# Three k decays moved to VectorE, and a new schedule of turns and loads, in a chunked linear-attention kernel with an MLP behind it

## The chip, the core and the metric

The kernel runs on one core of a Trainium2 chip. The core has TensorE (PE, matrix products into PSUM), VectorE (DVE), ScalarE (ACT), GpSimd (POOL) and SyncE (SP, here only a queue for DMAs). Each engine works through its own queue in order and waits on semaphores for the others. DMAs are asked for from SP's, ScalarE's and GpSimd's queues. The metric is the device time of one execution, in microseconds (us); lower is better.

## The reference

Four sequences of 768 tokens, 8 heads of 64. Each head has a decay `lam`; within a block of 64 tokens the scores are masked and decayed, and a state of 64 x 64 is carried from block to block. The result, 3072 tokens by 512, goes through an MLP with the activation h * tanh(softplus(h)).

```python
def _attn_ref(q, k, v, lam):
    ...
    for b in range(nb):
        sl = slice(b * block, (b + 1) * block)
        qb, kb, vb = (q[:, :, sl].copy(), k[:, :, sl].copy(), v[:, :, sl].copy())
        intra = np.einsum('bhic,bhjc->bhij', qb, kb) * Dmask[None]
        intra = np.einsum('bhij,bhjd->bhid', intra, vb)
        inter = np.einsum('bhid,bhde->bhie', qb * lam_pow[None], kv_state)
        out[:, :, sl] = intra + inter
        kb_dec = kb * rev_pow[None]
        kv_state = lam_block[None, :, None, None] * kv_state + np.einsum('bhsd,bhse->bhde', kb_dec, vb)
    return out.astype(np.float32)

def _moe_ref(x, w_in, w_out):
    h = x @ w_in
    sp = np.where(h > 20.0, h, np.log1p(np.exp(np.minimum(h, 20.0))))
    g = h * np.tanh(sp)
    return (g @ w_out).astype(np.float32)
```

`w_in` is 512 x 2048, `w_out` 2048 x 512. All inputs and the output are float32 in memory.

## The kernel before

The kernel works with blocks of C = 128 tokens. The state at a block's start carries everything before it, so the block size can be chosen freely. A **chunk** is one block of one of the four sequences, with all 8 heads; chunk i = 4n + b is block n of sequence b. The four chunks of a block make a **group** of 512 tokens; there are NG = 6 groups, n = 0 to 5.

**Stages.** The last loop of the kernel runs over n. Stage n does the MLP products of group n in **units**, and beside them the attention of group n + 1 in **pieces**, which are strewn among the units so that TensorE always has work. A stage from n = 1 on has 30 units: 16 (u = 0 to 15) for the first product with its activation (`mm1_unit`, tile `hsg`), and 14 (u = 16 to 29) for the second product (`fast_unit`: seven half-sized products in two halves each, in place of eight, with sums of tokens, `token_sum` into `gsum`, and of weights, `weight_sum` into `tsum`, made by VectorE). The first unit of stage n + 1 reads all of `xt[n + 1]`, the attention's output of the whole group.

**Pieces.** For groups from n = 2 on, a chunk has three pieces:
- `chunk_a`: TensorE makes k-transposed times v (`pv`), VectorE adds the old state (`raw`), GpSimd multiplies by the block's decay (`w`, the new state); then `turn(i + 2)` where that chunk is of the same group.
- `chunk_s`: TensorE makes the scores from `kraw` and `qraw` into two PSUM banks (tags pS and pk, one buffer each), VectorE masks them into `sb`.
- `chunk_o`: TensorE makes the output from `qraw` and the state, and from `sb` and v; VectorE scales it to `xtok`, and a DMA transpose asked for by SP turns it into `xt`.

Their order is a0 s0 a1 s1 o0 a2 s2 o1 a3 s3 o2 o3. The table `room` says how many pieces follow each unit. In stage 1 they stand at units 9 to 14 and 16 to 21, in later stages at units 4 to 19.

**Turns.** `turn(i)` has k multiplied by its decay (`scale_k`, tile `ktil`; by GpSimd for most chunks), and asks SP for two DMA transposes: q into `qraw`, then the decayed k into `kraw` (four buffers each). SP's queue holds these, the transposes of `xtok` and most output stores, in program order.

**Loads.** `load_k`, `load_q` and `load_v` are DMAs from float32 to float16 asked for by GpSimd, 128 KB each. Those of group 2 are asked for late in stage 0 and at its end. Stages 1 to 3 each ask for the twelve loads of the group two ahead, one at every second unit from u = 1 to 23. They stand in GpSimd's queue in one order with its decays and state updates; `kn`, `qn` and `vz` have eight buffers each.

**Order.** The schedule is written out by hand: each engine's instructions come in the order of the program. At a unit that order is: the unit's own instructions, a load from `later`, weight sums, token sums, a `turn` where one is due, then the pieces.

Lines that matter here: 261 (`scale_k`), 268 (`turn`), 377 (`chunk_a`, its `turn` at the end), 723 (`room`), 739 (`later`), 775 (the `turn` at unit 0 of stage 1). In the profile L264 is the decay, L273 the two turns of q and k, L384/L392/L394 are `pv`, `raw` and `w`, L406/L411 the scores and `sb`, L421/L425/L428/L429 the output, `xtok` and its turn, L482 the first MLP product, L541 `tsum`, L560 `gsum`, L587 the second product, and L69/L77/L80 the loads of k, q and v.

Of the kernel before, what the change touches and what calls it, by code (L numbers as in the profile page):

```python
# [13 lines left out]
def bc(ap, axis, n):  # L14
    shape = list(ap.shape)
    shape.insert(axis, n)
    return ap.unsqueeze(axis).broadcast_to(shape)
# [3 lines left out]
def kernel(  # L21
# [10 lines left out]
    nc = tc.nc  # L32
    B, H, S, D = q.shape
    C = 128
    NG = S // C
# [225 lines left out]
    def scale_k(i):  # L261

        t = work.tile([128, H, D], F16, name="ktil", tag="ktil", bufs=6)
        (nc.vector if i <= B or i >= (NG - 1) * B else nc.gpsimd).tensor_tensor(  # L264
            out=t, in0=kn[i], in1=bc(lk, 2, D), op=ALU.mult)
        ktil[i] = t

    def turn(i):

        scale_k(i)  # L270
        for src, name, to in ((qn, "qraw", qraw), (ktil, "kraw", kraw)):
            to[i] = work.tile([128, JP, C], F16, name=name, tag=name, bufs=4)
            nc.sync.dma_start_transpose(out=to[i], in_=src[i].rearrange("p h c -> p (h c)"))  # L273
# [103 lines left out]
    def chunk_a(s):  # L377

        n, b = s.n, s.b
        i = n * B + b  # L380
        if n < NG - 1:
            pv = ps.tile([128, JP, 128], F32, name="pv", tag=s.spare, bufs=2)
            for j in range(JP):
                nc.tensor.matmul(  # L384
                    pv[:, j, :].rearrange("p (a e) -> p a e", a=2),
                    ktil[i][:, 2 * j : 2 * j + 2, :].rearrange("p h c -> p (h c)"),
                    vz[i % NVB][:, 2 * j : 2 * j + 2, 0:D], start=True, stop=True,
                )
            for hf in range(2):
                raw = work.tile([128, 2, 128], F32, name="raw", tag="raw", bufs=3)  # L390
                hs = slice(2 * hf, 2 * hf + 2)
                nc.vector.tensor_tensor(  # L392
                    out=raw, in0=pv[:, hs, :], in1=wst[b][hf][n % 2], op=ALU.add)
                nc.gpsimd.tensor_tensor(  # L394
                    out=wst[b][hf][(n + 1) % 2], in0=raw, in1=lbm[:, hs, :], op=ALU.mult)
        if i + 2 < (n + 1) * B:
            turn(i + 2)

    def chunk_s(s):
# [32 lines left out]
    def chunk_pieces(n):  # L432
        chunks = []
        for b in range(B):
            s = Chunk()
            s.n, s.b = n, b
            chunks.append(s)
        out_ = []
        for t in range(B + 1):
            if t < B:  # L440
                out_ += [(chunk_a, chunks[t]), (chunk_s, chunks[t])]
            if t >= 1:
                out_.append((chunk_o, chunks[t - 1]))
        return out_
# [14 lines left out]
    def att_pieces(n):  # L459
        halves = att_halves(n)  # L460
        out_ = []
        for t in range(len(halves) + 2):
            if t < len(halves):
                out_.append((att_a, halves[t]))
            if 0 <= t - 1 < len(halves):
                out_.append((att_s, halves[t - 1]))
            if 0 <= t - 2 < len(halves):
                out_.append((att_o, halves[t - 2]))
        return out_
# [6 lines left out]
    def mm1_part(n, ni, lo, hi):  # L476

        if lo == 0:
            ph_t[ni] = ps.tile([128, GT], F32, name="ph", tag="po" if ni == 2 else "ph", bufs=2)
        w = DF // WS // 128  # L480
        for kc in range(NKC):
            nc.tensor.matmul(  # L482
                ph_t[ni][:, lo:hi],
                win0[min(ni, 2)][:, kc, max(ni - 2, 0) * 128 : max(ni - 2, 0) * 128 + 128] if ni < w
                else win[ni // w][:, kc, (ni % w) * 128 : (ni % w) * 128 + 128],
                xt[n][:, kc, lo:hi], start=(kc == 0), stop=(kc == NKC - 1),
            )
# [44 lines left out]
    def weight_sum(i, s):  # L532

        ks = slice(s * NKI // WS, (s + 1) * NKI // WS)
        a, b, op = (
            (w_quarter(0, 1, s), w_quarter(0, 0, s), ALU.subtract),
            (w_quarter(1, 1, s), tsum[0][:, ks, :], ALU.subtract),
            (w_quarter(1, 1, s), w_quarter(0, 1, s), ALU.subtract),
            (w_quarter(1, 0, s), tsum[1][:, ks, :], ALU.subtract),
        )[i]  # L540
        nc.vector.tensor_tensor(out=tsum[i][:, ks, :], in0=a, in1=b, op=op)  # L541
# [165 lines left out]
    for n in range(NG):  # L707
        units = [(mm1_unit, (n, ni)) for ni in range(NKI)]

        if n == 0:  # L710
            units += [(mm2_unit, (n, b2 + b, part)) for b2 in range(0, B, 2) for part in range(WS)
                      for b in range(2)]
        else:
            units += [(fast_unit, (n, step, blk)) for step in range(7) for blk in range(2)]
        pieces = []
        if n + 1 < NG:
            pieces = att_pieces(n + 1) if n + 1 < NT else chunk_pieces(n + 1)
        if n == 0:

            i = max(i for i, (f2, _) in enumerate(pieces) if f2 is att_a)  # L720
            pieces[i : i + 3] = pieces[i + 1 : i + 3] + pieces[i : i + 1]

        if n == 0:
            room = dict(zip(range(24, 32), (1, 2, 3, 3, 3, 3, 3, 3)))
        else:
            first = 8 if n == 1 else 3
            span = (22 if n == 1 else 20) - first
            room = {first + u: (u + 1) * len(pieces) // span - u * len(pieces) // span
                    for u in range(span)}
        if n == 1:  # L730

            for ni in range(3):
                mm1_part(n, ni, 0, GT - C)
                while late and ni < 2:
                    f2, s = late.pop(0)
                    f2(s)
                    if f2 is att_o:
                        break
        later = []
        if 1 <= n < NG - 2:  # L740
            later = [(lambda f=f, i=i: f(i)) for i in range((n + 2) * B, (n + 3) * B)
                     for f in (load_k, load_q, load_v)]
        nl = len(later)
        for u, (fn, args) in enumerate(units):
            rest = fn(*args)
            while later and u >= 1 and (nl - len(later)) * 24 <= (u - 1) * nl:
                later.pop(0)()
            if n == 0 and 19 <= u < 23:
                weight_sum(0 if u < 21 else 2, u % 2)
            if n == 1 and 4 <= u < 8:  # L750
                weight_sum(1 if u < 6 else 3, u % 2)
            if n > 0 and u in (9, 10):
                token_sum(n, 2, u - 9)
            if n > 0 and u == NKI - 3:
                token_sum(n, 0, 0)
            if n > 0 and u == NKI - 2:
                token_sum(n, 1, 0)
            if n > 0 and u == NKI - 1:
                token_sum(n, 0, 1)
                token_sum(n, 1, 1)  # L760
            if n > 0 and u in (NKI + 2, NKI + 3):
                token_sum(n, 3, u - NKI - 2)
            if n == 0 and 2 <= u < 2 + nh:
                att_kv(first_halves[u - 2], "po")
                att_w(first_halves[u - 2])
            if n == 0 and u % 2 == 1 and 0 < (u + 1) // 2 < B:
                scale_k((u + 1) // 2)
            if n == 0 and nh + 2 <= u < nh + 2 + NVB - B:
                nc.vector.memset(vz[u - nh - 2 + B][:, :, D : 2 * D], 0.0)
            if n == 0 and nh + 2 <= u < nh + 2 + NKB:  # L770
                nc.vector.memset(kz[u - nh - 2], 0.0)
            if n == 0 and u == 17:
                q_decays()
            if n == 0 and u == 16:
                nc.vector.tensor_scalar(out=maskT, in0=rel, scalar1=0.0, scalar2=None, op0=ALU.is_ge)
            if n == 0 and u == 18:
                scale_k(B)
            if n == 1 and u == 0:
                turn((n + 1) * B + 1)
            if n > 0 and n + 2 < NG and u in (23, 25):  # L780
                turn((n + 2) * B + (u - 23) // 2)
            for _ in range(room.get(u, 0)):
                f2, s = pieces.pop(0)
                s.spare = "po" if u < NKI - 1 else "ph"
                f2(s)
            if n == 0 and rest:
                rest()
        if n == 0:
            late = pieces
            while ahead:  # L790
                ahead.pop(0)()
# [30 lines left out]
```

## Time and profile before

| | us |
|---|---|
| three runs, median | 215.28 |
| the three runs | 217.44, 214.69, 215.28 |
| the profiled execution, time | 213.99 |
| the profiled execution, span | 211.8 |
| ScalarE busy in the span | 90.2 |

A page line such as `L394 POOL TENSOR_TENSOR w<-raw,lbm ... x24 | 18.6, 798 | ...` gives the line, the engine, the operation, the tile written and the tiles read, the count, the busy time in us, the mean in ns of one, and behind the second bar the engine's idle time ahead of these instructions and what ended it. In the timeline a line begins with the start (us from the span's beginning) and the duration; neighbours of one kind are merged, with their count at the end, and square brackets hold the idle time ahead and its releaser. Matmuls are pipelined, so of several merged ones the time to the next start is the better measure. In the view by window each engine's busy time in a stretch is followed by its count of instructions; the last three numbers are the granted TensorE clock, the share of the DMA engines and GB/s. "Issue" as a releaser means that the profile shows nothing that the engine waited for.

### The profile page before, as it was taken

Reading aid. Unit: us, or ns where it says so; the run is one execution under the profiler, and the core shown is the slowest. Engines: PE = TensorE matmul, PEld = TensorE weight load, DVE = VectorE, ACT = ScalarE, POOL = GpSimd, SP = SyncE. Lnnn points to the kernel's source line nnn. Section 1 sums busy time; section 2 is a strip of 40 time slices with the busy share of each in tenths; the row PEclk is TensorE's granted clock in tenths of the full one; section 3 lists DMA queues with packets and bytes.
Section 4 is the critical chain, followed back from the end, with each engine's and each line's share of the span. In section 5 each row is a group of like instructions: output and inputs, shape, how many; then the busy total and the mean of one; then the engine's idle time right before and its main releaser. Section 6 shows DMA issues by size and latency. Waiting matters only on the chain.

```text
span 211.8 us, 4225 instructions
## 1 busy us (share of the span) xinstructions
PE 198.4 (94%) x1672; PEld 127.8 (60%) x1672; DVE 127.9 (60%) x234; ACT 90.2 (43%) x159; POOL 110.6 (52%) x135
## 2 busy tenths in 40 slices
PE   7798999999997888989999999999999999999993
PEld 2465444577543477834579844579844588644893
DVE  6667560787715978616996517995727675222533
ACT  5474568466664321045532054532065521266310
POOL 7996333999899989608969409966000000000000
PEclk9999999999999999999999999999999999999998
DMA  9999999999999999994999994999963124400014
GB/s 133 141 158 178 206 207 185 155 198 73 179 144 163 134 101 125 138 242 78 118 136 66 163 264 69 112 129 82 234 160 74 25 28 99 152 0 0 2 56 145
DMA packets 112469, 26.75 MB, mean 126 GB/s; under 512 B 102594, under 2 KB 111938, under 8 KB 112450
## 3 DMA queue, kind: packets, MB, share of 16 engines
q0 software_dynamic: 78080, 13.37, 87.5%
q1 hardware_dynamic: 31392, 10.49, 25.7%
q10 hardware_dynamic: 2978, 2.62, 4.1%
q8 instruction: 13, 0.21, 0.4%
q14 instruction: 6, 0.05, 0.1%
HBM read 27.26 MB, written 6.29 MB: 158 GB/s over the span
## 4 chain that ended last, share of the span: by engine, by line
PE 75%; POOL 13%; DMA 6%; DVE 2%; issue 2%; POOLq 0%; DVEq 0%
PE ph L482 32%; PE z L587 13%; PE x L587 7%; PE y L587 7%; PE po L504 7%; DMA win<-in_moe_w_in_dram 4%; POOL kn L69 3%; POOL vz L80 3%; POOL qn L77 3%; DMA kraw<-ktil 2%; PE pS L406 2%; PE fin L587 2%; PE pO L425 2%; PE pO L421 1%; POOL ktil L264 1%
## 5 line engine op out<-in xcount | busy, mean ns | idle before, releaser
L482 PE MATMUL ph<-xt,win 128*128 128x512 f16 (+2 forms) x404 | 90.2, 369 | 2.4 <-issue 1.5
L496 ACT ACTIVATE hsg<-ph 128x512 f16<-128x512 f32 x96 | 57.0, 597 | 69.4 <-PE ph L482 69.3
L482 PEld LDWEIGHTS <-win 128*128 128x128 f16 x404 | 36.3, 98 | 38.9 <-issue 2.7
L587 PEld LDWEIGHTS <-gsum 128*128 128x128 f16 x336 | 31.1, 98 | 3.6
L394 POOL TENSOR_TENSOR w<-raw,lbm 128x256 f16<-128x256 f32 x24 | 18.6, 798 | 21.7 <-DVE raw L392 21.6
L560 DVE TENSOR_TENSOR gsum<-hsg 128x1024 f16<-128x1024 f16 x20 | 18.0, 913 | 13.2 <-ACT hsg L496 13.2
L411 DVE TENSOR_TENSOR sb<-pS,maskT 128x512 f16<-128x512 f32 x32 | 20.5, 683 | 8.1 <-PE pS L406 8.1
L587 PEld LDWEIGHTS <-hsg 128*128 128x128 f16 x240 | 22.9, 98 | 3.4
L77 POOL DMA_DIRECT2D qn<-in_q_dram x23 | 20.8, 904 | 5.5 <-DMA wout<-in_moe_w_out_dram 3.3
L80 POOL DMA_DIRECT2D vz<-in_v_dram x24 | 21.8, 910 | 3.4 <-DMA win<-in_moe_w_in_dram 1.7
L69 POOL DMA_DIRECT2D kn<-in_k_dram x23 | 21.2, 920 | 4.1 <-DMA wout<-in_moe_w_out_dram 1.7
L587 PE MATMUL z<-tsum,gsum 128*128 128x256 f16 x160 | 19.8, 273 | 0.0
L392 DVE TENSOR_TENSOR raw<-pv,w 128x256 f32<-128x256 f32 x24 | 9.1, 416 | 17.4 <-PE pv L384 15.5
L587 PE MATMUL x<-wout,hsg 128*128 128x256 f16 x160 | 19.4, 273 | 0.0
L264 POOL TENSOR_TENSOR ktil<-kn,lk 128x512 f16<-128x512 f16 x15 | 16.8, 1129 | 0.1
L504 PE MATMUL po<-wout,hsg 128*128 128x512 f16 x64 | 15.1, 379 | 0.0
L428 DVE TENSOR_TENSOR xtok<-pO,lqt 128x512 f16<-128x512 f32 x16 | 10.9, 683 | 0.0
L560 DVE TENSOR_TENSOR gsum<-hsg,gsum 128x1024 f16<-128x1024 f16 x10 | 7.6, 764 | 5.2 <-PE z L587 5.2
L264 DVE TENSOR_TENSOR ktil<-kn,lk 128x512 f16<-128x512 f16 (+1 forms) x9 | 6.2, 684 | 6.8 <-DMA kn<-in_k_dram 6.7
L425 PE MATMUL pO<-vz,sb 128*128 128x64 f16 x128 | 9.2, 193 | 0.8 <-DVE sb L411 0.8
L587 PE MATMUL z<-tsum,hsg 128*128 128x256 f16 x80 | 9.5, 272 | 0.0
L504 PEld LDWEIGHTS <-hsg 128*128 128x128 f16 x64 | 5.9, 97 | 5.9
(101 smaller groups left out, 226.5 us busy)
## 6 DMA issues: line engine op xcount, KB each, us to landing
out_dram<-osum SPq DMA_DIRECT2D x14, 256.0 KB, 3.1
vz<-in_v_dram POOLq DMA_DIRECT2D x24, 128.0 KB, 4.8
kn<-in_k_dram POOLq DMA_DIRECT2D x23, 128.0 KB, 5.1
qn<-in_q_dram POOLq DMA_DIRECT2D x23, 128.0 KB, 5.4
wout<-in_moe_w_out_dram POOLq DMA_DIRECT2D x4, 512.0 KB, 16.7
win<-in_moe_w_in_dram POOLq DMA_DIRECT2D x3, 512.0 KB, 10.4
out_dram<-osum ACTq DMA_DIRECT2D x5, 256.0 KB, 3.5
out_dram<-osb ACTq DMA_DIRECT2D x4, 256.0 KB, 5.5
```

What stands on the lines that cost most here:

```text
L69: nc.gpsimd.dma_start(out=kn[i], in_=chunk_rows(k, i))
L77: nc.gpsimd.dma_start(out=qn[i], in_=chunk_rows(q, i))
L80: nc.gpsimd.dma_start(out=vz[i % NVB][:, :, 0:D], in_=chunk_rows(v, i))
L264: (nc.vector if i <= B or i >= (NG - 1) * B else nc.gpsimd).tensor_tensor(out=t, in0=kn[i], in1=bc(lk, 2, D), op=ALU.mult)
L394: nc.gpsimd.tensor_tensor(out=wst[b][hf][(n + 1) % 2], in0=raw, in1=lbm[:, hs, :], op=ALU.mult)
L411: nc.vector.tensor_tensor(out=s.sb[t], in0=pS[t], in1=bc(maskT, 1, JP), op=ALU.mult)
L425: nc.tensor.matmul(psO[:, 2 * j + t, :], s.sb[t][:, j, :], vz[i % NVB][:, 2 * j + t, 0:D], start=False, stop=(t == 1))
L482: nc.tensor.matmul(ph_t[ni][:, lo:hi], win0[min(ni, 2)][:, kc, max(ni - 2, 0) * 128 : max(ni - 2, 0) * 128 + 128] if ni < w else win[ni // ...
L496: nc.scalar.activation(hsg[n][:, ni, :], ph_t.pop(ni), AF.Mish)
L504: nc.tensor.matmul(po, hsg[n][:, ki, b * C : (b + 1) * C], wout[part][:, kk, :], start=(ki == 0), stop=(ki == NKI - 1),)
L560: nc.vector.tensor_tensor(out=gsum[n, i][:, ks, :], in0=a, in1=b, op=op)
L587: nc.tensor.matmul(t, lhs(kk, b), rhs(kk, c, c + w), start=(fresh and kk == 0 and (alone or i == 0)), stop=(kk == HK - 1), skip_group_chec ...
```

## The change

Four edits, all in the schedule; what is computed stays the same.

1. `scale_k` runs on VectorE for chunks 9, 10 and 11 too (group n = 2 without its first chunk).
2. The turns of chunks 10 and 11 are no longer asked for in `chunk_a` of chunks 8 and 9; those of 9, 10 and 11 are asked for at units 0, 2 and 5 of stage 1.
3. In stage 1 the pieces are strewn from unit 7 on over 13 units instead of from 8 over 14. They then stand one to a unit, at units 8 to 19.
4. The twelve loads of stages 1 to 3 have fixed units, with none in units 14 to 20. In stage 1: 3, 5, 7, 9, 11, 13, 21, 22, 24, 26, 27, 28. In stages 2 and 3: 1, 2, 4, 5, 7, 8, 10, 11, 13, 21, 22, 23.

```diff
     def scale_k(i):
...
-        (nc.vector if i <= B or i >= (NG - 1) * B else nc.gpsimd).tensor_tensor(
+        (nc.vector if i <= B or 2 * B < i < 3 * B or i >= (NG - 1) * B else nc.gpsimd).tensor_tensor(
             out=t, in0=kn[i], in1=bc(lk, 2, D), op=ALU.mult)
...
     def chunk_a(s):
...
-        if i + 2 < (n + 1) * B:
+        if n > 2 and i + 2 < (n + 1) * B:
             turn(i + 2)
...
-            first = 8 if n == 1 else 3
-            span = (22 if n == 1 else 20) - first
+            first = 7 if n == 1 else 3
+            span = 20 - first
...
-        nl = len(later)
+        times = ((3, 5, 7, 9, 11, 13, 21, 22, 24, 26, 27, 28) if n == 1
+                 else (1, 2, 4, 5, 7, 8, 10, 11, 13, 21, 22, 23))
         for u, (fn, args) in enumerate(units):
             rest = fn(*args)
-            while later and u >= 1 and (nl - len(later)) * 24 <= (u - 1) * nl:
+            if later and u in times:
                 later.pop(0)()
...
-            if n == 1 and u == 0:
-                turn((n + 1) * B + 1)
+            if n == 1 and u in (0, 2, 5):
+                turn((n + 1) * B + 1 + u // 2)
             if n > 0 and n + 2 < NG and u in (23, 25):
                 turn((n + 2) * B + (u - 23) // 2)
```

## The prediction

> **What bounds the kernel now.** I began with the page's first part and then cut the span into stages with the view of busy time by window: the later part of the second group's matrix products (stage n=1) in two stretches, then stage n=2. Groups are counted from one in words, stages from zero: in stage n=1 the third group's chunks 8 to 11 have their attention.
>
> ```profile
> span 211.8 us, 4225 instructions
> PE 198.4 (94%) x1672; PEld 127.8 (60%) x1672; DVE 127.9 (60%) x234; ACT 90.2 (43%) x159; POOL 110.6 (52%) x135
> ...
> 62.00:84.00 22.00, 17.83 (x186) 12.01 (x185) 16.67 (x27) 6.92 (x12) 20.75 (x24) 1.00 1.75 134
> 84.00:91.00 7.00, 6.10 (x56) 5.21 (x55) 4.15 (x5) 0.00 (x0) 4.21 (x5) 1.00 1.93 132
> ...
> 91.00:122.00 31.00, 30.54 (x272) 20.30 (x270) 20.31 (x33) 11.34 (x19) 20.80 (x24) 1.00 1.38 134
> ```
>
> The columns are PE, PEld, DVE, ACT and POOL busy time. TensorE bounds the kernel: in the 31 us of stage n=2 it idles 0.46. Stage n=1 is the exception: between 62 and 84 us TensorE is idle 4.17 us, while VectorE is busy 16.67 and GpSimd 20.75 of 22. Next I read that stage in order of time on TensorE, for the idle time and its releasers.
>
> ```profile
> 63.28 0.39 PE L384 MATMUL pv<-vz,ktil 128*128 128x128 f16 x4
> 68.50 0.40 PE L406 MATMUL pS<-qraw,kraw 64*128 64x128 f16 x8 [1.58 <-DMA kraw<-ktil]
> 74.89 0.40 PE L406 MATMUL pS<-qraw,kraw 64*128 64x128 f16 x8 [1.74 <-DMA kraw<-ktil]
> 81.84 0.20 PE L425 MATMUL pO<-vz,sb 128*128 128x64 f16 x1 [0.45 <-DVE sb L411]
> 82.43 0.20 PE L425 MATMUL pO<-vz,sb 128*128 128x64 f16 x1 [0.40 <-DVE sb L411]
> 82.81 1.91 PE L587 MATMUL z<-tsum,gsum 128*128 128x256 f16 x16
> 84.56 1.91 PE L587 MATMUL y<-tsum,gsum 128*128 128x256 f16 x16
> 90.87 1.45 PE L482 MATMUL ph<-xt,win 128*128 128x512 f16 x6 [0.90 <-issue]
> 122.16 1.02 PE L482 MATMUL ph<-xt,win 128*128 128x512 f16 x4 [0.62 <-issue]
> ```
>
> There are three kinds of loss. The score products of chunks 9 and 10 wait for the turned k (1.58 + 1.74 us). Chunk 11's output products wait for its masked scores `sb` (0.45 + 0.40). Stage n=2 starts 0.90 late, stage n=3 0.62 late. The sum, 5.69 us or 2.6% of 215.28, is all that this change can win.
>
> The 0.90 is marked "issue", so I looked for what arrives just then. The SyncE queue's timeline shows the last two turns of the group's output, and the view of DMA issues gives the second one's landing.
>
> ```profile
> 83.00 2.58 SPq L429 DMA_TRANSPOSE xt<-xtok  x2
> ...
> xt<-xtok SPq DMA_TRANSPOSE x1, 6.5
> ```
>
> The second turn is issued near 84.3 and lands at 84.3 + 6.5 = 90.8; TensorE starts at 90.87. So stage n=2 begins at the later of two events: the end of n=1's products, and the landing of chunk 11's output turn.
>
> **The change part by part.** Why is k late? GpSimd's timeline, with the k loads of chunks 9, 11 and 12 (the last of the group after) and the decays of chunks 9, 10 and 11:
>
> ```profile
> 54.43 0.94 POOL L69 DMA_DIRECT2D kn<-in_k_dram  x1
> 59.71 0.93 POOL L69 DMA_DIRECT2D kn<-in_k_dram  x1
> 62.34 1.12 POOL L264 TENSOR_TENSOR ktil<-kn,lk 128x512 f16<-128x512 f16 x1
> 63.33 0.95 POOL L69 DMA_DIRECT2D kn<-in_k_dram  x1
> 67.75 1.46 POOL L394 TENSOR_TENSOR w<-raw,lbm 128x256 f16<-128x256 f32 x2
> 69.13 1.08 POOL L264 TENSOR_TENSOR ktil<-kn,lk 128x512 f16<-128x512 f16 x1
> 73.09 1.03 POOL L264 TENSOR_TENSOR ktil<-kn,lk 128x512 f16<-128x512 f16 x1
> ...
> kn<-in_k_dram POOLq DMA_DIRECT2D x1, 128.0 KB, 4.0
> kn<-in_k_dram POOLq DMA_DIRECT2D x1, 128.0 KB, 5.2
> kn<-in_k_dram POOLq DMA_DIRECT2D x1, 128.0 KB, 6.9
> ```
>
> The last three rows are times from issue to landing, of the k of chunks 9, 11 and 12. So k of chunk 9 is in SBUF at 58.4 and that of 11 at 64.9, but the decays of 9 and 11 run at 62.3 and 73.1, behind loads and state updates in GpSimd's queue.
>
> *Decays on VectorE, turns at units 0, 2, 5.* Removed from GpSimd: three decays, 1.12 + 1.08 + 1.03 = 3.2 us. The decays can run when k lands, so the waits of 1.58 and 1.74 us go: chunk 10's k turn can be issued near 64 instead of behind the decay at 69.13. What is late next is VectorE. Its queue runs in order, and unit 5's decay waits for chunk 11's k, which is only issued at 59.71. Queued behind it are the last two of four `tsum` sums, then chunk 8's `raw`, then chunk 8's `sb`; for `sb` wait chunk 9's scores (tag pS has one buffer) and chunk 8's output. VectorE's rows:
>
> ```profile
> 54.75 2.49 DVE L541 TENSOR_TENSOR tsum<-wout,tsum 128x1024 f16<-128x1024 f16 x4
> 63.77 0.76 DVE L392 TENSOR_TENSOR raw<-pv,w 128x256 f32<-128x256 f32 x2 [4.15 <-PE pv L384]
> 64.44 0.68 DVE L560 TENSOR_TENSOR gsum<-hsg 128x1024 f16<-128x1024 f16 x1
> 65.04 1.28 DVE L411 TENSOR_TENSOR sb<-pS,maskT 128x512 f16<-128x512 f32 x2
> 73.14 1.78 DVE L560 TENSOR_TENSOR gsum<-hsg 128x1024 f16<-128x1024 f16 x1
> 80.00 1.17 DVE L560 TENSOR_TENSOR gsum<-hsg,gsum 128x1024 f16<-128x1024 f16 x1
> 81.10 1.28 DVE L411 TENSOR_TENSOR sb<-pS,maskT 128x512 f16<-128x512 f32 x2
> 82.30 1.41 DVE L428 TENSOR_TENSOR xtok<-pO,lqt 128x512 f16<-128x512 f32 x2
> ...
> L264 DVE TENSOR_TENSOR ktil<-kn,lk 128x512 f16<-128x512 f16 (+1 forms) x9 | 6.2, 684 | 6.8 <-DMA kn<-in_k_dram 6.7
> ```
>
> Now VectorE is free until 63.77, when chunk 8's `raw` comes. Afterwards it is held until k of chunk 11 lands. That load shares the DMA engines with turns asked for earlier (k of 9, q and k of 10): 5.2 us is what it took with one turn beside it, 6.9 what chunk 12's took beside two. I take 6.2, nearer to the row with more turns, so it lands at 65.9 (64.9 to 66.6).
>
> From there to chunk 11's last `sb`, in start-to-start steps of these rows: one decay 0.68 (the mean of the last row); two `tsum` 2 x 0.62 = 1.24; eight `raw`, four pairs of 0.67 (63.77 to 64.44) = 2.68; eight `sb`, four pairs of 1.20 (81.10 to 82.30) = 4.80; six `gsum` at 0.60 (64.44 to 65.04) = 3.60; two `xtok` at 0.60 (by the row of `sb`, the same size) = 1.20. Sum 14.2 us. To it comes what GpSimd's work beside `gsum` costs. The `gsum` rows of 1.78 and 1.17 lie beside a decay (73.09) and a state update; against 0.68 they lost 1.1 and 0.5. The decays leave GpSimd, the updates stay: two of the six `gsum` follow a `raw` directly, 2 x 0.5 = 1.0, between 0 and 2.0.
>
> [...] For the decays I add nothing: the updates wait for `raw`, and all three decays stand ahead of `raw` in VectorE's order.
>
> Then chunk 11's `sb` ends at 65.9 + 14.2 + 1.0 = 81.1. On its way VectorE doesn't wait for TensorE, which needs 0.87 us for a unit and has fewer than 10 us of work between chunk 9's scores and chunk 11's output.
>
> *Pieces in units 8 to 19 instead of 9 to 21.* After chunk 11's output come ten half products, not eight. Two halves take 1.75 us (82.81 to 84.56), so 5 x 1.75 = 8.75 us. From the end of `sb` (81.10 + 1.28 = 82.38) to the next product (82.81) are 0.43. The products of n=1 end at 81.1 + 0.43 + 8.75 = 90.3. A gain of this move: chunk 11's `sb` now stands ahead of the last two `gsum`. The output turn: after `sb` come two `gsum` and two `xtok`, 4 x 0.60 + 0.1 = 2.5 us; issued at 83.6, with 6.5 to landing, 90.1. Both lie just ahead of 90.87: the stage wins 0.5 us. The stalls for k return as a stall of some 3 us for `sb` of chunk 8.
>
> *Loads pause in units 14 to 20.* This is a pause in program order. GpSimd has no clock of units; only the state updates, which wait for `raw`, hold it. In stage n=1 six loads of group 4 move behind chunk 11's update, so GpSimd issues them from about 82 on, as it issues loads there now. In stages n=2 and n=3 three loads remain behind the last update instead of four. The last output turn of n=2 may land a little earlier; of the 0.62 at 122.16 I take 0.2 (0 to 0.6). The moved loads cost nothing while the turns of group 4's k, needed only in n=2, have slack.
>
> Sum: -0.5 - 0.2 = -0.7 us. The profiled execution took 213.99 us, of which 211.8 are the span; the median of the three runs is 215.28, 1.29 above. From the median: 214.6.
>
> By the bounds: k of 11 at 63.7 (4.0 to landing) and no loss beside GpSimd give 63.7 + 14.2 + 9.18 = 87.1, 3.8 us ahead of 90.87. At 66.6 with a loss of 2.0, `sb` ends at 82.8; the products end at 92.0, and the output turn, issued 2.5 us after `sb` with 6.9, lands at 92.2: 1.3 late. So the forecast's own range is 213.0 to 216.6.
>
> **The rivals.** *All stalls go.* If VectorE isn't held (k of 11 lands before `raw` of chunk 8 is due), TensorE loses nothing and the 5.69 us go: 209.6. For it: the idle rows above name k and `sb`, and both are addressed. Against it: with a 4.0 us landing the hold still lasts until 63.7, and the sum above yields 3.8 at most, 4.4 with the 0.62. Chance 0.10.
>
> *A short hold.* k of 11 lands by 64, losses are small: -2.8 us, 212.5. For it: the row of 4.0. Against it: the row of 5.2, before any added turn. Chance 0.13.
>
> *The moved loads pile up on the output turns.* After chunk 11's update GpSimd issues six loads of group 4, two decays and three loads of group 5 without a stop, where it now issues three, two and two; these compete with the output turns of 10 and 11 and the q and k turns of 12 and 13. Four more loads at 0.88 us (59.71 to 62.34 holds three) are 3.5 us of DMA work. If the turn waits for all, it lands after 10 us instead of 6.5: 83.6 + 10.0 = 93.6, 2.7 us late. The turned k of group 4 then slips too, by up to the same 3.5, into n=2, which starts with less slack: 2.7 + 2.0 = 4.7 us slower, 220.0. It decides from a landing of 7.3 us (83.6 + 7.3 = 90.9). For it: the DMA share in 84 to 91 is already the highest, 1.93. Against it: the turns have a queue of their own, and the slowest k load beside them took 6.9. Chance 0.17.
>
> **How the numbers follow.** Forecast 0.60, the three rivals 0.10, 0.13 and 0.17. Two per cent, about what a measurement of this kernel can tell from no change, is 4.3 us: faster than 211.0 or slower than 219.6. Faster: the first rival, 0.10, since the sum's own best end hardly reaches it. Slower: most of the third, 0.14. Within: 0.76. The range takes in the forecast's range, the second rival and the lower part of the third: 212.3 to 217.5; beyond it lie the first rival and some half of the third, under 0.2.
>
> **What would show it.** Right: no wait for turned k in n=1; instead an idle VectorE ended by the k load until about 65.9, a TensorE stall of some 3 us ahead of chunk 9's scores or chunk 8's output, chunk 11's `sb` ending near 81, stage n=2 starting at 90 to 91. Wrong: VectorE's decay of chunk 11 before 63.5 or after 67, a start of n=2 before 88 or after 92, an output turn of chunk 11 landing after more than 7.3 us, or new idle time of TensorE in n=2 and n=3.

## The result

The changed kernel takes 215.52 us (median of 20 executions, 211.86 to 216.28), the kernel before 216.18 (20 executions, 214.69 to 218.41), a ratio of 0.9969. Each ratio with an interval below is taken over the executions that lie within about 1.5% of their kernel's fastest (here 7 of the 20 after), so it can differ from the ratio of the medians, which take in all. That ratio is 0.9887, 95% interval 0.9847 to 0.9927; a second comparison on another chip gave medians of 214.53 and 216.13 (0.9926) and a ratio of 0.9972 (0.9928 to 1.0015). By these four figures the change is worth 0.3% to 1.1%, within the 2% of "no change"; one of the two intervals takes in no change at all.

The profile after is of an execution of 216.09 us, span 214.2. Two spans can't simply be subtracted: the second group's first unbroken run of full-width products begins at 57.24 us in the profile before and at 58.95 in the one after, and two profiles of one kernel differ there by as much. So I count each stage from its first full-width product:

| us | start of n=1 | n=1 | n=2 | n=3 | n=4 |
|---|---|---|---|---|---|
| before | 57.24 | 33.63 | 31.29 | 30.50 | 29.62 |
| before, second profile | 58.82 | 33.90 | 31.66 | 31.50 | 29.61 |
| after | 58.95 | 35.11 | 30.50 | 30.51 | 29.61 |
| after, second profile | 57.17 | 34.83 | 30.98 | 30.67 | 29.61 |

Stage n=1, which the change was mostly about, is 1.2 us *longer*; stages n=2 and n=3, in which only the loads' units changed, are shorter by 0.7 and 0.4 us on the mean of two. These three add up to nothing. A small part of the gain lies outside the profile's span altogether: time less span is 1.81 to 1.90 us in all 32 executions of the changed kernel and 2.14 to 2.29 in the 56 of the kernel before in the three comparisons of the experiments, some 0.35 us less; nothing on record says what it is. Here is stage n=1 of the profile after on TensorE, in order of time:

```profile
64.13 0.39 PE L384 MATMUL pv<-vz,ktil 128*128 128x128 f16 x4
...
72.81 0.26 PE L406 MATMUL pS<-qraw,kraw 64*128 64x128 f16 x1 [5.04 <-DVE sb L411]
73.41 0.58 PE L406 MATMUL pS<-qraw,kraw 64*128 64x128 f16 x7 [0.34 <-DVE sb L411]
73.92 1.89 PE L482 MATMUL ph<-xt,win 128*128 128x512 f16 x4
...
76.47 1.11 PE L482 MATMUL ph<-xt,win 128*128 128x512 f16 x4
...
78.93 1.04 PE L482 MATMUL ph<-xt,win 128*128 128x512 f16 x4
...
80.26 1.04 PE L587 MATMUL x<-wout,hsg 128*128 128x256 f16 x8
```

Both waits for turned k and both waits ahead of chunk 11's output are gone. In their place stands one wait of 5.04 + 0.34 = 5.4 us ahead of chunk 9's scores, released by `sb`. VectorE, timeline of the same stretch, says why:

```profile
63.41 0.69 DVE L264 TENSOR_TENSOR ktil<-kn,lk 128x512 f16<-128x512 f16 x1 [2.44 <-DMA kn<-in_k_dram]
64.02 1.29 DVE L541 TENSOR_TENSOR tsum<-wout,tsum 128x1024 f16<-128x1024 f16 x2
68.57 0.69 DVE L264 TENSOR_TENSOR ktil<-kn,lk 128x512 f16<-128x512 f16 x1 [3.27 <-DMA kn<-in_k_dram]
69.18 1.29 DVE L541 TENSOR_TENSOR tsum<-wout,tsum 128x1024 f16<-128x1024 f16 x2
70.38 0.75 DVE L392 TENSOR_TENSOR raw<-pv,w 128x256 f32<-128x256 f32 x2
71.05 1.10 DVE L560 TENSOR_TENSOR gsum<-hsg 128x1024 f16<-128x1024 f16 x1
72.08 1.27 DVE L411 TENSOR_TENSOR sb<-pS,maskT 128x512 f16<-128x512 f32 x2
...
83.39 1.28 DVE L411 TENSOR_TENSOR sb<-pS,maskT 128x512 f16<-128x512 f32 x2
```

VectorE sits idle for 3.27 us, ended by a DMA (the k of chunk 11), while TensorE's products for chunk 8's `raw` have been there since about 64.5. The page and the view by window show a second thing that the page before doesn't have (the row of the clock before, then the one after, and the windows after):

```profile
PEclk9999999999999999999999999999999999999998
...
PEclk9999999999999589999999999999999999999999
...
68.00:70.00 2.00, 0.00 (x0) 0.09 (x1) 1.43 (x3) 0.40 (x1) 0.00 (x0) 0.95 2.53 152
70.00:72.00 2.00, 0.00 (x0) 0.00 (x0) 2.00 (x4) 0.00 (x0) 1.11 (x2) 0.50 1.83 155
74.00:75.00 1.00, 1.00 (x3) 0.35 (x4) 1.00 (x3) 0.00 (x0) 0.62 (x1) 0.50 1.73 42
77.00:78.00 1.00, 1.00 (x9) 0.60 (x8) 1.00 (x3) 0.38 (x1) 0.56 (x1) 1.00 0.69 44
```

The third number from the right is the granted clock. In this profile it falls to 0.50 within the idle time and stays there into the work that follows. A unit and a chunk's output take 76.47 - 73.92 = 2.55 us there, and 80.26 - 78.93 = 1.33 later: 1.2 us lost, beside some 0.25 in the scores ahead of them. That is TensorE's time; what of it shows in the stage's length is taken up below.

Last, the output turns. For each kernel, the two that end stage n=1 (SyncE's timeline, and the view by line with least, median and longest time to landing); before first, then after:

```profile
83.00 2.58 SPq L429 DMA_TRANSPOSE xt<-xtok  x2
...
DMA to landing us min/median/max: 6.0/6.2/6.5
```

```profile
86.98 2.95 SPq L429 DMA_TRANSPOSE xt<-xtok  x2
...
DMA to landing us min/median/max: 3.7/4.3/4.8
```

They land about 2 us sooner after their issue, and stage n=2 no longer starts late. The sooner landing isn't general, though: with the loads alone, whose units are the same new ones, both took 5.8 us, and what the loads change is better seen in stage n=2, below.

### The profile page after: what moved, and what is told of

Same layout as the page of the kernel before. It is cut to its first block, busy times and chain, and to the rows that moved or that the text cites. A ratio compares the mean times of both kernels' runs of the same rounds, so it can differ in the third digit from the quotient of the medians.

```text
span 214.2 us, 4219 instructions
## 1 busy us (share of the span) xinstructions
PE 201.6 (94%) x1672; PEld 130.2 (61%) x1672; DVE 130.0 (61%) x237; ACT 90.2 (42%) x159; POOL 107.9 (50%) x132
## 4 chain that ended last, share of the span: by engine, by line
PE 84%; DMA 5%; DVE 5%; POOL 3%; issue 1%; ACT 0%; ACTq 0%; DVEq 0%
PE ph L482 35%; PE z L587 12%; PE x L587 8%; PE y L587 7%; PE po L504 6%; DMA kn<-in_k_dram 3%; PE pS L406 2%; DMA qn<-in_q_dram 2%; PE pO L425 2%; PE pO L421 2%; PE fin L587 2%; PE pO L249 1%; PE pv L384 1%; PE busy L165 1%; PE pS L235 1%
## 5 line engine op out<-in xcount | busy, mean ns | idle before, releaser
L482 PE MATMUL ph<-xt,win 128*128 128x512 f16 (+2 forms) x404 | 91.2, 371 | 0.4 <-ACT hsg L496 0.2
L587 PEld LDWEIGHTS <-hsg 128*128 128x128 f16 x240 | 23.0, 98 | 2.9
L560 DVE TENSOR_TENSOR gsum<-hsg 128x1024 f16<-128x1024 f16 x20 | 17.1, 868 | 11.5 <-ACT hsg L496 11.5
L264 DVE TENSOR_TENSOR ktil<-kn,lk 128x512 f16<-128x512 f16 (+1 forms) x12 | 8.2, 687 | 14.4 <-DMA kn<-in_k_dram 14.4
L264 POOL TENSOR_TENSOR ktil<-kn,lk 128x512 f16<-128x512 f16 x12 | 13.6, 1136 | 0.1
L406 PE MATMUL pS<-qraw,kraw 64*128 64x128 f16 x128 | 6.8, 223 | 5.4 <-DVE sb L411 5.4
L406 PEld LDWEIGHTS <-kraw 64*128 64x128 f16 x128 | 3.9, 96 | 11.4 <-issue 9.3
L560 DVE TENSOR_TENSOR gsum<-hsg,gsum 128x1024 f16<-128x1024 f16 x10 | 8.1, 817 | 3.3 <-PE z L587 3.3
L165 PE MATMUL busy<-kzero 128*128 128x512 f16 x18 | 8.5, 573 | 1.2 <-DVE kzero L150 1.2
```

The source lines that it names most:

```text
L264: (nc.vector if i <= B or 2 * B < i < 3 * B or i >= (NG - 1) * B else nc.gpsimd).tensor_tensor(out=t, in0=kn[i], in1=bc(lk, 2, D), op=ALU. ...
L406: nc.tensor.matmul(pS[t][:, j, :], kraw[i][rs, j, :], qraw[i][rs, j, :], start=True, stop=True)
L482: nc.tensor.matmul(ph_t[ni][:, lo:hi], win0[min(ni, 2)][:, kc, max(ni - 2, 0) * 128 : max(ni - 2, 0) * 128 + 128] if ni < w else win[ni // ...
L560: nc.vector.tensor_tensor(out=gsum[n, i][:, ks, :], in0=a, in1=b, op=op)
L587: nc.tensor.matmul(t, lhs(kk, b), rhs(kk, c, c + w), start=(fresh and kk == 0 and (alone or i == 0)), stop=(kk == HK - 1), skip_group_chec ...
```

## The experiments

The first four experiments move the turns, fill the long idle time, or move the decays back. There were three groups of four, each on a chip of its own with the kernel before beside it; so across groups the ratios compare better than the times.

**Chunk 11's turn at unit 10.** The decay that waits is put behind chunk 8's `raw` and `sb`.

```diff
-            if n == 1 and u in (0, 2, 5):
-                turn((n + 1) * B + 1 + u // 2)
+            if n == 1 and u in (0, 2, 10):
+                turn((n + 1) * B + 1 + (0, 2, 10).index(u))
```

> Only the turn of chunk 11 moves, from unit 5 to unit 10, so that its decay stands behind chunk 8's raw and masked scores in VectorE's queue. Theory A (the hold: VectorE waits for chunk 11's k with chunk 8's work queued behind it): chunk 8's masked scores end near 67 us instead of 73.3, TensorE's idle time ahead of chunk 9's scores falls from 5.4 us to under 2, the granted clock stays at 1.00 between 62 and 84 us, and the time falls by 3 to 5 us against the changed kernel, to 211 to 212.5. Theory B (VectorE has too much work in stage n=1, wherever the wait stands): the idle time only moves to a later piece and the time stays within 1 us of the changed kernel.

212.12 us (6 executions), ratio 0.9834 (0.9794 to 0.9874). TensorE's idle time ahead of chunk 9's scores is 1.44 + 0.27 = 1.7 us, stage n=1 lasts 31.56 us. Theory A holds; theory B falls, since VectorE does the same work here. Two expectations failed: chunk 8's `sb` ends at 69.8 instead of near 67, because VectorE still waits 2.56 us for chunk 10's k, and the clock dips in this profile too (0.50 from 70.5 to 73.5 us).

**Turns at units 0, 7 and 10.** As above with `(0, 7, 10)`.

> The turns of chunks 10 and 11 move to units 7 and 10, so that the four weight sums run ahead of chunk 10's decay too. Theory A: another 0.5 to 1.5 us less idle time ahead of chunk 9's scores than with units 0, 2, 10, since 2.4 us of weight sums go into VectorE's wait for chunk 9's and 10's k; 210 to 211.5. Theory B: the same as with units 0, 2, 5. If chunk 10's or 11's turned k comes too late, TensorE shows a wait for it ahead of the scores of 10 or 11.

210.66 us (209.67 to 211.42), ratio 0.9771 (0.9736 to 0.9807): the fastest kernel of the study. VectorE does all four weight sums ahead of chunk 10's decay, and neither this decay nor that of chunk 11 waits at its place in the queue:

```profile
60.13 2.49 DVE L541 TENSOR_TENSOR tsum<-wout,tsum 128x1024 f16<-128x1024 f16 x4
62.73 0.69 DVE L264 TENSOR_TENSOR ktil<-kn,lk 128x512 f16<-128x512 f16 x1
63.84 0.76 DVE L392 TENSOR_TENSOR raw<-pv,w 128x256 f32<-128x256 f32 x2 [0.42 <-PE pv L384]
...
67.85 0.68 DVE L264 TENSOR_TENSOR ktil<-kn,lk 128x512 f16<-128x512 f16 x1
```

TensorE then idles 1.19 us ahead of chunk 9's scores and 0.54 ahead of chunk 10's, both for turned k, so the idle time is no less than with chunk 11's turn moved alone (1.73 against 1.71): that part of the expectation failed. Stage n=1 lasts 30.11 us, and the clock stays at 0.998 or above in all six executions.

**Matmuls on zeros in the idle time.** 18 matmuls whose results nobody reads, ahead of chunk 9's scores:

```diff
     def chunk_s(s):

         i = s.n * B + s.b
+        if i == 2 * B + 1:
+            busy(18)
```

> 18 matmuls of 512 columns on zeros, 3.9 us at 0.215 each, are put on TensorE ahead of chunk 9's scores, where it idles 5.4 us; nothing else of the changed kernel is altered. Theory C (the long idle time halves the clock for the products that follow, and costs about 1.5 us): the granted clock stays at 1.00 from 70 to 77 us instead of 0.50, and the time is 1 to 2 us below the changed kernel, about 214. If the clock is no consequence of the idle time: the clock falls as before and the time is the same, or up to 1 us longer where the hold is shorter than the added matmuls.

The mean clock is 0.998 or more in all 11 executions; in the two comparisons of the changed kernel it was below 0.993 in 30 of 32. (In the kernel before, whose profiles show no dip, it was below 0.993 in 12 of 56; the mean doesn't say where in the span a dip lies.) With TensorE kept busy, the same wait for `sb` no longer ends in a slow clock (1.00 in all five windows of 2 us from 66 to 76). The added lines move the line numbers by two, so L408 is L406:

```profile
65.82 4.05 PE L165 MATMUL busy<-kzero 128*128 128x512 f16 x18
70.11 0.21 PE L408 MATMUL pS<-qraw,kraw 64*128 64x128 f16 x1 [0.24 <-DVE sb L413]
70.70 0.38 PE L408 MATMUL pS<-qraw,kraw 64*128 64x128 f16 x7 [0.39 <-DVE sb L413]
71.02 1.04 PE L484 MATMUL ph<-xt,win 128*128 128x512 f16 x4
```

So the dip is a consequence of the idle time. Its price doesn't show in the time: 214.91 us, ratio 0.9918 (0.9876 to 0.9960), where the changed kernel has 215.52 and 214.53. Stage n=1 is 33.83 us, 1.0 to 1.3 shorter than in the two profiles after, but chunk 11's output waits 0.41 + 0.40 us for `sb` again: VectorE, not TensorE, is then what is late. Of the 1.0 us against the second profile after, which starts the stage at the same 57.17, 0.6 are no matter of the clock: chunk 11's decay starts at 65.86 instead of 66.43. So the 1.2 us rest on the rows of the profile after, as time of TensorE, and what the clock costs the kernel is smaller and not measured by itself.

**Decays back on GpSimd, turns early.** Edit 1 undone.

```diff
-        (nc.vector if i <= B or 2 * B < i < 3 * B or i >= (NG - 1) * B else nc.gpsimd).tensor_tensor(
+        (nc.vector if i <= B or i >= (NG - 1) * B else nc.gpsimd).tensor_tensor(
```

> The decays of chunks 9 to 11 go back to GpSimd; the turns stay at units 0, 2 and 5. Theory A: VectorE is not held, chunk 8's raw starts near 63.8 us; GpSimd waits for k instead, and only loads and state updates queue behind it. TensorE has no idle time ahead of chunk 9's scores over 1 us, and the time is 211 to 213. Theory B' (it is early turns as such, whose transfers delay the loads of k): the stall stays at 3 us or more and the time is 214 to 216.

212.59 us, ratio 0.9812 (0.9761 to 0.9863), stage n=1 30.88 us. Chunk 8's `raw` isn't held; it waits for its product. TensorE's idle time ahead of chunk 9's scores is 1.61 us, more than expected, and for turned k. So early turns alone do not make the stall, and VectorE isn't needed for the decays.

The next experiments take single parts.

**The loads alone.** Edit 4 on the kernel before (and the condition that reads it):

```diff
-        nl = len(later)
+        times = ((3, 5, 7, 9, 11, 13, 21, 22, 24, 26, 27, 28) if n == 1
+                 else (1, 2, 4, 5, 7, 8, 10, 11, 13, 21, 22, 23))
```

> Only the new units of the loads (edit 4) on the kernel before; decays, turns and pieces as before. By the prediction it moves little: in stage n=1 four loads instead of five stand ahead of chunk 8's state update and chunk 10's decay in GpSimd's queue, so chunk 10's turned k comes about 0.9 us earlier, and stage n=3 may start 0.2 us earlier: 0.5 to 1.5 us faster than before. If the moved loads pile up on the output turns (the prediction's third rival), stage n=2 starts late and the time is 2 to 4 us slower than before.

212.60 us against 216.57, ratio 0.9817 (0.9775 to 0.9859): 4.0 us faster, where 0.5 to 1.5 were expected. By its ratio this one part is faster than the whole change (0.9887 and 0.9972), though its interval just touches that of the first. Stages n=1, n=2 and n=3 last 32.15, 30.73 and 30.51 us. The second profile of the kernel before, taken for this question with its code unchanged, shows what the loads remove:

> The kernel before, unchanged, for a second profile. With the loads' old units the profiles so far have a stage n=3 of 30.5, 31.0 and 31.6 us and a stage n=2 of 30.8 to 31.3; with the new units n=3 is 30.5 each time. If the old units make late output turns in stages n=2 and n=3 (theory L), this profile shows idle time at the starts of stages n=3 or n=4 again, 0.5 us or more in sum; if the first profile's stage lengths are the rule, 31.3 and 30.5.

TensorE's timeline, the first products of stages n=2, n=3 and n=4; the second profile before, then the loads alone:

```profile
92.72 4.48 PE L482 MATMUL ph<-xt,win 128*128 128x512 f16 x20 [1.11 <-issue]
124.38 4.48 PE L482 MATMUL ph<-xt,win 128*128 128x512 f16 x20 [0.98 <-issue]
...
155.88 5.34 PE L482 MATMUL ph<-xt,win 128*128 128x512 f16 x24 [0.84 <-issue]
```

```profile
75.17 0.40 PE L406 MATMUL pS<-qraw,kraw 64*128 64x128 f16 x8 [0.68 <-DMA kraw<-ktil]
...
90.55 4.48 PE L482 MATMUL ph<-xt,win 128*128 128x512 f16 x20 [0.30 <-issue]
```

Before, three stages start late, by 1.11 + 0.98 + 0.84 = 2.9 us; the first profile had 0.90 + 0.62 and nothing at n=4, and was a lucky draw (213.99 us, where the medians are 216). With the new loads, stage n=2 starts 0.30 late, n=3 and n=4 not at all, and chunk 10's scores wait 0.68 us instead of 1.74. Theory L holds, and the other profiles bear it out: in all five profiles with the old units (the two before, pieces alone, old loads, turns and decays alone) the late starts add up to 1.4 to 2.9 us, in the nine with the new ones this 0.30 is the only one.

How the late starts come about is seen in stage n=2, where no stall shifts anything. The last output turn is issued 24.2 to 24.3 us after the stage's start in both profiles before and in the first after; the stage's products last 30.5 us, so by these figures a landing more than some 6.2 us after the issue makes the next stage late. Before, it landed after 6.9 and 7.3 us, in the first profile after within 5.7. First and second profile before, then after, the last two output turns of stage n=2 by line:

```profile
L429 SPq DMA_TRANSPOSE xt<-xtok x2: 1190/1216/1242, 113.7 to 115.2; - x2
...
DMA to landing us min/median/max: 5.2/6.0/6.9
...
L429 SPq DMA_TRANSPOSE xt<-xtok x2: 1201/1245/1289, 115.6 to 117.0; - x2
...
DMA to landing us min/median/max: 5.6/6.4/7.3
...
L429 SPq DMA_TRANSPOSE xt<-xtok x2: 1192/1257/1322, 116.9 to 118.3; - x2
...
DMA to landing us min/median/max: 5.4/5.5/5.7
```

That it is one load fewer close behind the last state update which makes the difference fits the order in GpSimd's queue (four loads in a row before, three after), but wasn't tested by itself.

The new units aren't free: in five of the nine profiles with them a chunk's scores in stage n=2 wait 0.17 to 0.67 us for turned k, in none of the five with the old ones.

**The pieces alone.** Edit 3 on the kernel before.

```diff
-            first = 8 if n == 1 else 3
-            span = (22 if n == 1 else 20) - first
+            first = 7 if n == 1 else 3
+            span = 20 - first
```

> Only the earlier pieces (edit 3) on the kernel before. Chunk 10's scores then stand at unit 14 instead of 16 while their turned k still comes late behind GpSimd's queue: TensorE's wait for it grows by about 1 to 1.7 us, and the wait of 0.85 us ahead of chunk 11's output goes. From 0.5 us faster to 1.5 us slower than before. If the pieces' place alone were what the changed kernel wins by, it would be 1 us faster or more.

Not resolved: a median of 217.15 us against 216.57, but a ratio of 0.9871 (0.9817 to 0.9925), which rests on two of the six executions, 213.22 and 214.06; the other four took 217.01 or more. The profile has 3.56 us of idle time ahead of chunk 9's scores, for turned k, where a longer wait for chunk 10's was expected; the clock dips (a mean of 0.84 over 62 to 84 us, where the kernel before has 1.00), and the mean clock of the execution lies below 0.993 in four of six executions. The waits ahead of chunk 11's output are gone, as expected. A gain of its own isn't shown.

**The old loads in the changed kernel.** Edit 4 undone.

```diff
-        times = ((3, 5, 7, 9, 11, 13, 21, 22, 24, 26, 27, 28) if n == 1
-                 else (1, 2, 4, 5, 7, 8, 10, 11, 13, 21, 22, 23))
+        nl = len(later)
...
-            if later and u in times:
+            while later and u >= 1 and (nl - len(later)) * 24 <= (u - 1) * nl:
                 later.pop(0)()
```

> The changed kernel with the old units of the loads (edit 4 undone). The hold on VectorE stays, since the loads of group 3's own k are untouched: an idle time of TensorE of 4 to 6 us ahead of chunk 9's scores, time within 1 us of the changed kernel. If the pause is what carries the changed kernel's gain, it is 1.5 us slower or more, with the output turn of chunk 11 landing after stage n=1's last product.

217.01 us against 216.57, ratio 1.0018 (0.9983 to 1.0052). Edits 1 to 3 together bring nothing. The profile has late starts of 0.92 us at n=2 and at n=4, and the wait of 3.79 + 0.38 us for `sb`. The idle time is as expected; of the time, the second case came true: against the kernel before this is 0.5% to 1.3% worse than the changed kernel, and the last output turn of n=1 lands late.

**Turns and decays alone.** Edits 1 and 2 on the kernel before.

```diff
-        (nc.vector if i <= B or i >= (NG - 1) * B else nc.gpsimd).tensor_tensor(
+        (nc.vector if i <= B or 2 * B < i < 3 * B or i >= (NG - 1) * B else nc.gpsimd).tensor_tensor(
...
-        if i + 2 < (n + 1) * B:
+        if n > 2 and i + 2 < (n + 1) * B:
...
-            if n == 1 and u == 0:
-                turn((n + 1) * B + 1)
+            if n == 1 and u in (0, 2, 5):
+                turn((n + 1) * B + 1 + u // 2)
```

> Only edits 1 and 2 on the kernel before: the three decays on VectorE and the turns at units 0, 2, 5; pieces and loads as before. Theory A: the hold stays, and chunk 9's scores stand one unit later (unit 12 instead of 11), so TensorE's idle time ahead of them is about 0.9 us less than with the pieces at 8 to 19, 3 to 4.5 us; two fewer units follow chunk 11's output. Stage n=1 lasts 33 to 35 us, the time is within 2 us of before, and no faster than the loads alone (212.6). If these two edits are what makes the changed kernel faster, they alone give 1% or more.

218.95 us against 216.13, ratio 1.0132 (1.0071 to 1.0193): 2.8 us slower, where within 2 was expected. Stage n=1 is 36.71 us, not 33 to 35. TensorE waits 4.23 + 0.39 us for chunk 8's `sb` and again 0.45 + 0.39 us ahead of chunk 11's output, and stages n=2 and n=4 start 1.01 and 0.55 us late.

**The k loads first.** The changed kernel with another order of the third group's loads:

```diff
-        (lambda f=f, i=i: f(i)) for i in range(2 * B, 3 * B) for f in (load_k, load_q, load_v)
+        (lambda f=f, i=i: f(i)) for f, i in (
+            (load_k, 8), (load_q, 8), (load_v, 8), (load_k, 9), (load_k, 10), (load_k, 11),
+            (load_q, 9), (load_v, 9), (load_q, 10), (load_v, 10), (load_q, 11), (load_v, 11))
```

> The changed kernel with turns at units 0, 2, 5, but the k loads of chunks 10 and 11 are asked for ahead of q and v of chunk 9: chunk 11's k load moves from the tenth to the sixth place of the twelve, 4 x 0.88 = 3.5 us earlier. If the hold is the wait for that load, VectorE's last decay starts about 3 us earlier after the stage's beginning, TensorE's idle time ahead of chunk 9's scores falls from 5.4 us to 1.5 to 2.5, the granted clock dips seldom, and the time is 212 to 213. If what holds VectorE is its own work, or the turns in flight, the idle time stays above 4 us and the time at 215 to 216.

213.93 us, ratio 0.9812 (0.9756 to 0.9868). The hold goes: chunk 11's decay starts at 63.24 instead of 68.57 (the stage starts within 0.2 us of the other). But a wait of 3.48 us stands at the same place, now for turned k, so the idle time and the time missed what was expected. SyncE's queue shows it: q of chunk 9 is loaded later, its turn waits until 63.42, and chunk 9's k turn, whose data had been ready since about 61.3, stands behind it.

```profile
63.42 1.19 SPq L273 DMA_TRANSPOSE qraw<-qn  x1
64.71 1.29 SPq L273 DMA_TRANSPOSE kraw<-ktil  x1
```

**Turns at 0, 7, 10 with the old pieces.** Edit 3 undone in the fastest kernel.

```diff
-            first = 7 if n == 1 else 3
-            span = 20 - first
+            first = 8 if n == 1 else 3
+            span = (22 if n == 1 else 20) - first
```

> Turns at units 0, 7 and 10 with the decays on VectorE and the new units of the loads, but the pieces at units 9 to 21 as before (edit 3 undone). Chunk 9's scores then wait less for their turned k (1.19 us idle with pieces at 8 to 19), but chunk 11's masked scores stand behind the last token sum again and are waited for by 0.7 to 0.9 us, and two fewer units cover the last output turn. Stage n=1 within 0.7 us of 30.1; 210 to 211.5. If the pieces' move is worth something by itself, 1 us slower than with them moved, 211.5 to 212.

212.04 us, ratio 0.9857 (0.9800 to 0.9915), 1.4 us slower than with the pieces moved, on another chip; stage n=1 31.43 us, 1.3 longer where 0.7 was expected. Chunk 9's scores wait 1.60 + 0.38 us for `sb`, not less than with the pieces moved, and chunk 11's output 0.45 + 0.40 us, as expected. Not all of the loss is the pieces' own: with the old units, the turn at unit 10 comes ahead of chunk 8's `sb` in VectorE's queue. There the decay took 2.38 us, beside chunk 8's state update on GpSimd:

```profile
65.62 2.38 DVE L264 TENSOR_TENSOR ktil<-kn,lk 128x512 f16<-128x512 f16 x1
...
65.92 1.51 POOL L394 TENSOR_TENSOR w<-raw,lbm 128x256 f16<-128x256 f32 x2
```

**The changed kernel again**, on the chip of the last group.

> The changed kernel once more, beside the others on one chip: 213.5 to 216.5, with an idle time ahead of chunk 9's scores of 3.5 to 5.5 us and a granted clock below 1.00 in most executions. Where an execution keeps the clock at 1.00, the span is 2 us or more shorter.

214.53 us (213.27 to 216.55), ratio 0.9972 (0.9928 to 1.0015), as expected: the idle time is 4.68 + 0.39 us, the mean clock below 0.993 in all twelve executions. So none kept its clock, and the last condition stays without a case here; the two of the first 20 executions after that did took 211.86 and 213.20 us.

## Why the prediction was right, and where it was not

The time lies in the range, and the step from before to after, -0.66 us between the medians, is almost the -0.7 of the forecast. That closeness is luck: the stage that the change was mostly about came out about 2 us longer than worked out, and the part that was put at 0.2 us won about five times that.

By the prediction's own signs the account of stage n=1 failed, if narrowly. Counted from its start and set beside the profile before, stage n=2 begins at 92.35 and 92.07 us in the two profiles after, where 90 to 91 was to show it right and after 92 to show it wrong.

- **The hold of VectorE: right in mechanism, too small.** The chain ran as worked out: decay, two `tsum`, `raw`, `gsum`, `sb`. From chunk 11's decay to its last `sb` the sum gave 14.2 + 1.0 = 15.2 us; measured were 16.1 (68.57 to 84.67), of which 0.89 was a wait for TensorE, which the prediction had ruled out. The rest of the chain is 15.2, as summed. The mis-sized term is the landing of chunk 11's k: 6.2 us taken, 6.9 as the upper end, 7.1 and 6.8 in the two profiles after. In the first of them the decay starts 1.0 us later in the stage than forecast; with the 0.89 and 0.2 behind the last `sb` that is the whole difference between the forecast stage (90.3 - 57.24 = 33.1) and the measured 35.1. "A stall of some 3 us" became 5.4 and 5.1; it was too low by the prediction's own terms, which put the end of chunk 8's `sb` at 65.9 + 0.68 + 1.24 + 0.67 + 0.60 + 1.20 = 70.3, some 4 us behind the point at which TensorE comes to chunk 9's scores with the pieces one unit earlier (68.50 - 1.58 = 66.92 in the profile before, less 0.87 for a unit).
- **The clock: missing.** I priced the stall as idle time alone. The profile before, with idle times up to 1.74 us in this stage, shows no dip, and I didn't ask what a longer one would do. It cost TensorE about 1.4 us more, by the rows of the profile after; the zeros show that the idle time is its cause. In the stage's length it shows as at most the 0.89 us that VectorE waits for chunk 8's output, made under the slow clock: the rest of the stage hangs on VectorE.
- **The pieces' move: as forecast** for chunk 11's `sb`, which is no longer waited for in the two profiles after.
- **The pause of the loads: the step that failed.** "This is a pause in program order", with 0.2 us (0 to 0.6) for a late start, undersold the one edit that wins. With the new units the last two output turns of stage n=2 land sooner, after 5.4 to 5.7 and 4.3 to 5.2 us in the two profiles after, where the two before had 5.2 to 6.9 and 5.6 to 7.3. And 0.62 us, a single execution's late start, was no measure of what there was to win: it is 1.4 to 2.9 us over the stages. "The moved loads cost nothing" was a little too good: in the second profile after, a chunk's scores in stage n=2 wait 0.41 us for turned k.
- **The sum.** -0.5 for stage n=1 became +1.2 on the mean of two profiles each; -0.2 for the later stages became -1.1 (-0.7 and -0.4). To that come the 0.35 us outside the span. What is left of the gain isn't resolved by so few profiles; the medians say -0.7 and -1.6 us. The range's lower end, 213.0, doesn't follow from the bound that is given for it: 3.8 us below 215.28 is 211.5.
- **The rivals.** "The moved loads pile up on the output turns" falls: the loads alone are 1.8% faster. "A short hold" falls too: k of chunk 11 landed later than the likeliest value, not earlier. "All stalls go" comes near once VectorE isn't held: 210.66 us with the turns at units 0, 7 and 10, with 1.73 us of idle time left.
- **The decay's price beside GpSimd.** I charged nothing because the decays stand ahead of `raw`. In the changed kernel that held (0.69 us each). With the turns at units 0, 7 and 10 and the old pieces one decay stands behind `raw`, with a state update beside it, and took 2.38 - 0.68 = 1.7 us longer than a decay in the profile before. That the update is the cause isn't shown: the decay is listed as starting first (65.62 against 65.92).

## What to carry to other kernels

Work moved to an idle engine brings its wait along (here 3.27 us for chunk 11's k): before an operation is put early into an in-order queue, ask when its data lands and what is queued behind it; here the same decay asked for five units later made the kernel over 2 us faster by the medians. Price a TensorE stall of several microseconds with the slow clock after it (here 0.50, for 3.4 and 6.8 us in the two profiles after), as far as the work that follows waits for TensorE. And where one profile shows a small late start at a stage's border, take a second profile before calling it small: prefetches that are early enough anyway were cheap here, though not quite free (waits of 0.17 to 0.67 us for turned k), to move away from the transfers that a stage's start waits for.

## What the runs showed of the hardware

By windows of half a microsecond the clock's dip to 0.50 lasted 6.8 us in the first profile after (69.8 to 76.6), and 3.4 us in the second profile after, with chunk 11's turn at unit 10, with the old loads, and with turns and decays alone. With the pieces alone and with the k loads first the clock over 62 to 84 us has a mean of 0.84, as in the first profile after. In the five profiles with these windows the dip begins within the idle time or up to 0.4 us behind its end. The length of the idle time alone doesn't decide: with chunk 11's turn at unit 10, 1.44 + 0.27 = 1.7 us of idle time (with one matmul within) were followed by a dip in the profile, while 1.83 us in the second profile before and 1.60 + 0.38 us with the turns at 0, 7, 10 and the old pieces were not (1.00 over 62 to 84 us in both). (How many of the unprofiled executions had such a dip can't be read from their mean clock: the profile of the loads alone has a mean of 0.984, and 1.00 in every window from 52 to 184 us.)

A load of 128 KB with conversion from float32, asked for by GpSimd, took 4.0 us to land where no turn was asked for within its time (chunk 9's k before) and 7.1 where three were, and a fourth 0.3 us ahead of it (chunk 11's k after). The output turns that end stage n=1, in their own queue, took 6.0 to 6.5 us before, where the first of them was issued 1.3 us behind the first of three loads in a row. With the new units decays stand between these loads, but that alone isn't what makes the turns quick: where the first turn came 2.4 us behind the first load, in the two profiles after (87.0 against 84.58 and 84.9 against 82.52), they took 3.4 to 5.1 us, and where it came 1.3 us behind, with the loads alone (83.3 against 81.99), 5.8.
